# Tracing VectorE's attention work as one stream ahead of the weights' steps, with one product of the norm moved to ScalarE

## The chip, the cores and the metric

The kernel runs on one core of one Trainium2 chip. The metric is the device time of one execution in microseconds (us). Beside plain runs there is one profiled execution, whose trace is read here; its times are those of one execution. Engines are called as the profile calls them: PE is TensorE, DVE is VectorE, ACT is ScalarE, POOL is GpSimd and SP is SyncE, which issues most of the transfers.

## The reference: what is computed

A linear attention with a complex, normed gate runs over 768 time steps, for 4 batches and 8 heads of width 48. Its output is then the input of a mixture of four experts, whose results are summed with weights.

```python
mag = np.sqrt(a_re * a_re + a_im * a_im)
scale = np.minimum(mag, 0.999) / (mag + 1e-06)
a_re_n, a_im_n = (a_re * scale, a_im * scale)
for t in range(S):
    new_re = ar * S_re - ai * S_im
    new_im = ar * S_im + ai * S_re
    kv = np.einsum('bhd,bhe->bhde', k[:, :, t], v[:, :, t])
    S_re, S_im = (new_re + kv, new_im)
    y[:, :, t] = np.einsum('bhd,bhde->bhe', q[:, :, t], S_re)
...
p = d / (d.sum(-1, keepdims=True) + 1e-09)
for e in range(E):
    out += p[:, e:e + 1] * (np.maximum(x @ w1[e], 0.0) @ w2[e])
```

Here x is y with its heads side by side: 3072 rows of 384 numbers. An expert is 384 to 1024 to 384.

## The kernel before, in words

**Blocks.** The 3072 rows are worked off as NG = 12 blocks of G = 256 rows, each in two chunks of 128. A matrix product in fp32 is made of three products of high and low parts (hi x hi, lo x hi, hi x lo), so every x, hidden value and weight exists as a pair (xha and xla, hh and hl, whi and wlo).

**Two phases.** Up to about 614 us the experts 0 and 1 are applied to one block after the other (`moe1`, `mo.block`), and the attention of the next block is worked off between their steps. Then experts 2 and 3 run on blocks of 512 rows (`w1_full`, L739, and `w2_full`, L752) without any attention beside them. The change touches the first phase alone.

**A weight's step.** Each block takes eight steps of two weight tiles. `w1_step` makes 18 products into ph (L172); ScalarE makes hh from it (Relu, L181) and VectorE hl (L182). `w2_step` of the step before then makes 12 products into po (L191), from hh and hl. Ahead of each step k the function `between(k)` is called, which traces the pieces of the next block's attention; FIRST (L60) says with which step k the first of the three pieces comes.

**The attention of a block g.** Its gates are first normed (`norm`, L305 to L332): two Squares on ScalarE, their sum on VectorE, Ln, Exp and Identity on ScalarE, four products on VectorE (L326, L327, L328, L330) with a Square for a check between, and the product with the gates A. `prefix` (L334 to L356) then forms products of gates over the time steps of a chunk (pf, then sk and fm). The `head` of `finish` (L398) forms the squared magnitude of these products, its Ln and Exp, and Q (L408) out of q; the `tail` (L416) forms K (L422) out of k, with the inverse. `trip` (L428) writes Q or K to memory (q_d, k_d, L432) and reads it back turned round into Qst or Kst (L437), both on SP's queue.

TensorE's own pieces follow: turning K (ktp, L466, copied into KT), the increment of the state (dp, L484, then G on VectorE), the scores (sc, L496, out of Qst and Kst, then masked by VectorE into scs, L499), the values (yp, L510 and L515, copied into y by ScalarE, L522). At the end of a block `t_factors` copies TA and TB out of Qst (L444 to L447), and `rotate` (L534 to L537) turns the state G with them. For the blocks 0, 1 and 2 (XSEL = 3) the output is turned round on TensorE (xp, L546) and split into xha and xla straight from there (L159, L161); from block 3 on it goes through memory (`store_y`, `load_x`). Block 1 (and 0) is near: its K of the first chunk is turned on TensorE and copied into Kst by ScalarE (kp, L475, L476).

**What sets the order.** On each engine the instructions run in one fixed order. It is found by a scheduler that plays the program through when it is built; it starts from the order in which the code traces the instructions, and lets one pass another where its own clock says that this one is ready. In the kernel before, `front(g + 1)` (prefix, head, tail and the trips of a whole block) and `norm(g + 2)` are traced in one piece behind all eight steps of block g - 1. Tiles come from pools: gates A from two buffers, the temporaries of norm, prefix and Q from one pool of four (TMP), K from one.

Of the kernel before, what the change touches and what calls it, by code (L numbers as in the profile page):

```python
# [8 lines left out]
F32 = mybir.dt.float32  # L9
# [50 lines left out]
FIRST = {1: 5, 2: 4, 3: 3, 4: 2}  # L60
# [5 lines left out]
def fast_path(ctx, tc, qkP, aP, vP, probsP, w, out, flag):  # L66
# [16 lines left out]
    nc.vector.memset(neg1, -1.0)  # L83
    one1 = const.tile([P, 1], F32, name="one1")
# [137 lines left out]
    with ExitStack() as c1:  # L222
# [82 lines left out]
        def norm(g, A, parts=((0, SEG),), prev=(None, None)):  # L305
            s = tmp(f"s{g}")
            u = tmp(f"u{g}")
            for n, (lo, hi) in enumerate(parts):
# [15 lines left out]
                exp = nc.scalar.activation(y0, L, AF.Exp, scale=-0.5)
                idn = nc.scalar.activation(L, y0, AF.Identity, scale=-EPS, bias=one1)
                nc.vector.tensor_tensor(v, m2, y0, op=ALU.mult)  # L326
                nc.vector.scalar_tensor_tensor(v, v, 2.0 * EPS, y0, op0=ALU.add, op1=ALU.mult)  # L327
# [4 lines left out]
            return idn  # L332

        def prefix(g, A, cuts=(1, NS)):  # L334
            for i in range(1, SEG):
# [6 lines left out]
                nc.vector.tensor_tensor(x[:, 1], z[:, 1, 0], z[:, 0, 1], op=ALU.add)  # L342
            Al = A[:, :, SEG - 1, :]
            As = A.rearrange("p c i (j s) -> p c i j s", j=NJ)
            k = 1
            for lo, hi in zip(cuts, cuts[1:]):
                while k < hi:
# [3 lines left out]
                    cmul(Ak[:, :, :, k:], br, bi, [nb, k], f"sk{g}_{k}")  # L351
                    k *= 2
# [3 lines left out]
                yield  # L356
# [279 lines left out]
        nrm = norm(0, A[0], parts=halves)  # L636
        cuts = (1, NS // CG, NS)

        def front(g, A, qk):
            pre = prefix(g, A, cuts if g < NSEL else (1, NS))  # L640
            Q, K, head, tail = finish(g, A, qk)
            if g >= NSEL:
                next(pre, None)
                la = head(0, CG)
                ld = tail(0, CG)
                backs = [trip(f"{nm}_d{g}", X, st) for nm, X, st in (("q", Q, Qst), ("k", K, Kst))]
                return (Q, K), la, ld, [back() for back in backs][-1], None
# [10 lines left out]
            if g > 0:  # L658
                tail(0, 1)
# [318 lines left out]
```

## Time and profile before

| what | us |
|---|---|
| median of 3 runs | 1030.87 |
| lowest and highest run | 1030.55 and 1032.13 |
| profiled execution | 1026.41 |
| its span (first to last instruction) | 1024.5 |
| VectorE busy | 599.0 |
| ScalarE busy | 356.0 |

The profiled execution is 1.9 us longer than its span, and 4.46 us below the median. The granted TensorE clock over the span was 0.988 of full speed. A row of the timeline gives start, duration, engine, line, operation and tiles, and in brackets for how long its engine had been idle and on whom it waited; xN are neighbours of one kind put together. In the list of waits the three numbers are the sum, the number of waits and the longest. Names of tiles in the profile have no block number; which block a row belongs to comes from its place in the order.

### The profile page before, as it was taken

What the parts mean: (1) busy time and instruction counts of PE and PEld (TensorE: products, weight loads), DVE (VectorE), ACT (ScalarE), POOL (GpSimd) and SP (SyncE); (2) the same over time, 40 slices, a digit from 0 to 9 for tenths busy, and PEclk for the clock granted to TensorE, in tenths of its full rate; (3) what the DMA queues carried; (4) which work ended last, traced back from release to release, by engine and by line L of the source; (5) the groups of instructions that cost most, each with busy time, mean ns of one, the idle gap of its engine ahead of it and who ended that gap; (6) DMA issues with size and microseconds to landing.
All of it is one profiled execution on the core that took longest, in us unless ns stands there. A gap on an engine that the chain in (4) does not pass through costs nothing.

```text
span 1024.5 us, 16293 instructions
## 1 busy us (share of the span) xinstructions
PE 991.4 (97%) x6688; PEld 930.6 (91%) x6688; DVE 599.0 (58%) x1219; ACT 356.0 (35%) x642; POOL 34.3 (3%) x64
## 2 busy tenths in 40 slices
PE   4899999998999999999999999999999999999997
PEld 2799989898999999999999999989999999999996
DVE  7897979787888989788872264232232232321221
ACT  7655525353453536436242353121111111211110
POOL 5020000000000000000000000000000000000000
PEclk9899999998999999999999999999999999999999
DMA  9465265564736547384461592011030110100000
GB/s 325 137 131 148 86 163 132 132 161 125 191 116 167 142 130 187 123 201 121 120 167 29 187 337 94 1 62 62 1 123 1 31 62 1 62 1 1 32 1 34
DMA packets 74131, 110.78 MB, mean 108 GB/s; under 512 B 5248, under 2 KB 58544, under 8 KB 74048
## 3 DMA queue, kind: packets, MB, share of 16 engines
q1 hardware_dynamic: 69760, 94.53, 32.9%
q0 software_dynamic: 4288, 15.13, 5.0%
q8 instruction: 54, 0.88, 0.4%
q14 instruction: 29, 0.24, 0.1%
HBM read 73.72 MB, written 35.92 MB: 107 GB/s over the span
## 4 chain that ended last, share of the span: by engine, by line
PE 92%; DVE 2%; DMA 2%; issue 1%; ACT 1%; DVEq 0%; ACTq 0%
PE pob L752 20%; PE phb L739 19%; PE ph L172 19%; PE po L191 18%; PE sc L496 5%; PE dp L484 3%; PE yp L515 2%; PE yp L510 2%; PE ktp L466 1%; PE xp L546 1%; DMA Qst<-q_d 1%; DMA Kst<-k_d 1%; PE qp L368 0%; PE kp L368 0%; PE lp L142 0%
## 5 line engine op out<-in xcount | busy, mean ns | idle before, releaser
L745 DVE SCALAR_TENSOR_TENSOR hlb<-phb,hhb 128x512 fp32r<-128x512 f32 x96 | 66.3, 691 | 246.7 <-ACT hhb L744 246.7
L744 ACT ACTIVATE hhb<-phb 128x512 fp32r<-128x512 f32 x96 | 57.4, 598 | 313.3 <-PE phb L739 299.0
L191 PE MATMUL po<-whi,hh 128*128 128x384 f32 x384 | 129.4, 340 | 0.0
L752 PE MATMUL pob<-wlo,hhb 128*128 128x384 f32 x384 | 129.3, 337 | 0.0
L191 PE MATMUL po<-wlo,hh 128*128 128x384 f32 x384 | 129.1, 336 | 0.0
L752 PE MATMUL pob<-whi,hhb 128*128 128x384 f32 x384 | 128.9, 336 | 0.0
L191 PE MATMUL po<-whi,hl 128*128 128x384 f32 x384 | 123.9, 338 | 0.0
L752 PE MATMUL pob<-whi,hlb 128*128 128x384 f32 x384 | 117.8, 336 | 0.0
L172 PE MATMUL ph<-xha,whi 128*128 128x256 f32 x576 | 104.8, 288 | 0.6 <-ACT xha L159 0.6
L172 PE MATMUL ph<-xha,wlo 128*128 128x256 f32 x576 | 102.5, 284 | 0.0
L172 PE MATMUL ph<-xla,whi 128*128 128x256 f32 x576 | 102.4, 285 | 0.0
L181 ACT ACTIVATE hh<-ph 128x512 fp32r<-128x512 f32 x96 | 57.2, 596 | 130.0 <-PE ph L172 120.9
L182 DVE SCALAR_TENSOR_TENSOR hl<-ph,hh 128x512 fp32r<-128x512 f32 x96 | 66.0, 688 | 58.5 <-ACT hh L181 58.2
L739 PE MATMUL phb<-xhb,whi 128*128 128x512 f32 x288 | 91.8, 392 | 0.0
L172 PEld LDWEIGHTS ph<-xha,whi 128*128 128x128 f32 x576 | 87.2, 192 | 1.9 <-ACT xha L159 1.1
L172 PEld LDWEIGHTS ph<-xla,whi 128*128 128x128 f32 x576 | 83.2, 191 | 0.5 <-issue 0.5
L172 PEld LDWEIGHTS ph<-xha,wlo 128*128 128x128 f32 x576 | 83.5, 191 | 0.0
L739 PE MATMUL phb<-xlb,whi 128*128 128x512 f32 x288 | 83.4, 392 | 0.0
L739 PE MATMUL phb<-xhb,wlo 128*128 128x512 f32 x288 | 82.1, 393 | 0.0
L752 PEld LDWEIGHTS pob<-wlo,hhb 128*128 128x128 f32 x384 | 72.1, 188 | 3.5
L752 PEld LDWEIGHTS pob<-whi,hhb 128*128 128x128 f32 x384 | 72.1, 188 | 3.4
L191 PEld LDWEIGHTS po<-whi,hh 128*128 128x128 f32 x384 | 72.4, 189 | 0.6 <-issue 0.5
(165 smaller groups left out, 1585.3 us busy)
## 6 DMA issues: line engine op xcount, KB each, us to landing
wst<-w SPq DMA_DIRECT2D x25, 384.0 KB, 5.9
qk<-qkP SPq DMA_DIRECT2D x24, 384.0 KB, 6.8
acc_d<-acc POOLq DMA_DIRECT2D x24, 384.0 KB, 4.0
prev<-acc_d SPq DMA_DIRECT2D x24, 384.0 KB, 5.1
q_d<-Q SPq DMA_DIRECT2D x22, 387.0 KB, 3.5
Qst<-q_d SPq DMA_DIRECT2D x22, 387.0 KB, 5.8
A<-aP SPq DMA_DIRECT2D x22, 384.0 KB, 8.0
k_d<-K SPq DMA_DIRECT2D x20, 384.0 KB, 2.9
```

What stands on the lines that cost most here:

```text
L172: ins = nc.tensor.matmul(ph[:, u, :], wt[:, j * P:(j + 1) * P], xt[:, j, :], start=(n == 0), stop=(n == 3 * NJ - 1))
L181: wts["hh"] = nc.scalar.activation(hh, ph, AF.Relu)
L182: nc.vector.scalar_tensor_tensor(hl, ph, 0.0, hh, op0=ALU.max, op1=ALU.subtract)
L191: nc.tensor.matmul(po[t], ht[:, u, t * P:(t + 1) * P], wt[:, HD:], start=(i % FE == 0 and n == 0), stop=(i % FE == FE - 1 and n == 2))
L484: nc.tensor.matmul(d_ps[:, h, :], KT[:, h, :], vc[:, h * D:(h + 1) * D], start=True, stop=True)
L496: nc.tensor.matmul(s_ps[:, h, :], Kc[:, hf * 4 + h, :], Qc[:, hf * 4 + h, :], start=True, stop=True)
L510: ins = nc.tensor.matmul(yo, st[:, o:o + n], Qc[:, o // D, :], start=True, stop=False)
L515: ins = nc.tensor.matmul(yo, vc[:, o:o + n], sc[h // 4][:, h % 4, :], start=first, stop=True)
L739: nc.tensor.matmul(ph, wt[:, j * P:(j + 1) * P], xt[:, j, :], start=(n == 0), stop=(n == 3 * NJ - 1))
L744: nc.scalar.activation(hh, ph, AF.Relu)
L745: nc.vector.scalar_tensor_tensor(hl, ph, 0.0, hh, op0=ALU.max, op1=ALU.subtract)
L752: nc.tensor.matmul(po[t], ht[:, t * P:(t + 1) * P], wt[:, HD:], start=(i % FE == 0 and n == 0), stop=(i % FE == FE - 1 and n == 2))
```

## The change

It makes generators of `norm`, `prefix` and `front`: after each portion they yield a cost in us. `stream()` runs front(g) and norm(g + 1) for g = 1 to 11, one behind the other, and `advance(us, upto)` takes portions from it worth `us`, up to block `upto`. `between(k)` calls it ahead of every step of weights with STEP = 3.4 us, and with MORE on top at the three steps that carry a piece of attention. FIRST is raised by one for the blocks 2, 3 and 4. For the blocks in HALF (2 and 3) tail and K's trip are done chunk by chunk, which makes two writes and two reads of half the size out of each.

In the norm the factor 0.5 * CAP goes into Exp's bias. For g > 0 the two products m2 * y0 and (v + 2 EPS) * y0 of VectorE become a Square of y0 on ScalarE and one product of VectorE; the clamp becomes a max with -1, followed by the product with an Identity that has the other sign.

```diff
-FIRST = {1: 5, 2: 4, 3: 3, 4: 2}
+FIRST = {1: 5, 2: 5, 3: 4, 4: 3}
+STEP = 3.4
+MORE = (1.9, 1.9, 0.5)
+HALF = (2, 3)
...
-                exp = nc.scalar.activation(y0, L, AF.Exp, scale=-0.5)
-                idn = nc.scalar.activation(L, y0, AF.Identity, scale=-EPS, bias=one1)
-                nc.vector.tensor_tensor(v, m2, y0, op=ALU.mult)
-                nc.vector.scalar_tensor_tensor(v, v, 2.0 * EPS, y0, op0=ALU.add, op1=ALU.mult)
+                exp = nc.scalar.activation(y0, L, AF.Exp, scale=-0.5, bias=lnb)
+                if g == 0:
+                    nc.vector.tensor_tensor(v, m2, y0, op=ALU.mult)
+                    nc.vector.scalar_tensor_tensor(v, v, 4.0 / CAP ** 2, y0, op0=ALU.mult, op1=ALU.mult)
+                else:
+                    nc.scalar.activation(v, y0, AF.Square, scale=2.0 / CAP)
+                    nc.vector.tensor_tensor(v, m2, v, op=ALU.mult)
+                nc.scalar.activation(L, y0, AF.Identity, scale=2.0 * EPS / CAP, bias=neg1)
+                yield 0.95
                 nc.vector.scalar_tensor_tensor(y0, v, 3.0, y0, op0=ALU.subtract, op1=ALU.mult)
+                yield 0.95
                 nc.scalar.activation(v, v, AF.Square, bias=neg1, accum_out=st_w[:, col:col + 1])
-                nc.vector.scalar_tensor_tensor(y0, y0, -0.5 * CAP, L, op0=ALU.mult, op1=ALU.min)
+                nc.vector.scalar_tensor_tensor(y0, y0, -1.0, L, op0=ALU.max, op1=ALU.mult)
...
+            if g in HALF:
+                kb = []
+                for c in range(CG):
+                    last["dve"] = tail(c, c + 1)
+                    yield 2.7
+                    kb.append(trip(f"k_d{g}_{c}", K, Kst, c, c + 1))
+                    if c == 0:
+                        qb()
+                for back in kb:
+                    last["q"] = back()
...
+        def stream():
+            for g in range(1, NG):
+                qk = load_qk(g, last["q"])
+                if g + 1 < NG:
+                    A.append(load_a(g + 1, prev=last["q"]))
+                for r in front(g, A[g], qk):
+                    yield g, r
+                if g + 1 < NG:
+                    for r in norm(g + 1, A[g + 1]):
+                        yield g, r
+
+        work = stream()
+        spent = {"g": 1, "us": 0.0}
+
+        def advance(us, upto):
+            spent["us"] -= us
+            while spent["us"] < 0 and spent["g"] <= upto:
+                r = next(work, None)
+                if r is None:
+                    spent["g"] = NG
+                    return
+                spent["g"], cost = r
+                spent["us"] += cost
...
+            def between(k, g=g, first=first, end=end):
+                advance(STEP + (MORE[k - first] if first <= k <= end else 0.0), g + 1)
...
+                if g < NG and first <= k <= end:
+                    while g not in todo:
+                        advance(0.5, g)
...
-            if g + 1 < NG:
-                qk = load_qk(g + 1, landed)
-                if g + 2 < NG:
-                    A.append(load_a(g + 2, prev=landed))
-                QK, la, ld, landed, todo[g + 1] = front(g + 1, A[g + 1], qk)
-                if g + 1 >= NSEL:
-                    todo[g + 1] = attention(g + 1, QK)
-                if g + 2 < NG:
-                    norm(g + 2, A[g + 2])
```

TensorE's instructions stay the same in number. ScalarE gets 11 Squares, VectorE loses one product per norm and gains eight halves, and SP gets eight transfers more. How the order moves is shown at three places; in a name like hh0_7 the first number is the block and the second the step, in u23 it is temporary u2 of block 3 and in s4 temporary s of block 4.

ScalarE, where block 1's first scores need Kst. Before:

```order
L324 ACTIVATE u2_773<-s2_772 128x768
L444 ACTIVATE TA_164<-Qst_160 48x8
L445 ACTIVATE TA_164<-Qst_160 48x8
L325 ACTIVATE s2_772<-u2_773,one1_85 128x768
L446 ACTIVATE TB_165<-Qst_160 48x8
L447 ACTIVATE TB_165<-Qst_160 48x8
L476 ACTIVATE Kst_161<-kp1_0_0_988 112x4x128
L476 ACTIVATE Kst_161<-kp1_0_4_994 112x4x128
L181 ACTIVATE hh0_7_1239<-ph0_7_1220 128x512
```

The same place now:

```order
L330 ACTIVATE u2_967<-s2_966,lnb_85 128x768
L459 ACTIVATE TA_166<-Qst_162 48x8
L460 ACTIVATE TA_166<-Qst_162 48x8
L461 ACTIVATE TB_167<-Qst_162 48x8
L335 ACTIVATE u2_967<-u2_967 128x768
L337 ACTIVATE s2_966<-u2_967,neg1_83 128x768
L462 ACTIVATE TB_167<-Qst_162 48x8
L491 ACTIVATE Kst_163<-kp1_0_0_981 112x4x128
L491 ACTIVATE Kst_163<-kp1_0_4_987 112x4x128
L186 ACTIVATE hh0_7_1267<-ph0_7_1248 128x512
```

The norm's new Square and its Identity stand behind the first TB copy, where the Identity stood ahead of it.

ScalarE, where block 2's x is copied into xha. Before:

```order
L159 ACTIVATE xha2_1733<-xp2_1_1689 128x3x128
L405 ACTIVATE u23_1781<-s23_1780,a2b_89 128x24x16
L411 ACTIVATE Q3_1782<-A3_1258 128x12
L313 ACTIVATE s4_1871<-A4_1777 128x768
L314 ACTIVATE s4_1871<-A4_1777 128x768
L405 ACTIVATE u23_1781<-s23_1780,a2b_89 128x24x16
L406 ACTIVATE u23_1781<-u23_1781,a2e_91 128x24x16
L181 ACTIVATE hh2_0_1904<-ph2_0_1885 128x512
L406 ACTIVATE u23_1781<-u23_1781,a2e_91 128x24x16
L323 ACTIVATE s4_1871<-s4_1871,m2b_87 128x768
L181 ACTIVATE hh2_1_1945<-ph2_1_1926 128x512
L324 ACTIVATE u4_1872<-s4_1871 128x768
```

The same place now:

```order
L420 ACTIVATE u23_1647<-s23_1646,a2b_91 128x24x16
L426 ACTIVATE Q3_1648<-A3_1054 128x12
L318 ACTIVATE s4_2039<-A4_1643 128x768
L319 ACTIVATE s4_2039<-A4_1643 128x768
L420 ACTIVATE u23_1647<-s23_1646,a2b_91 128x24x16
L164 ACTIVATE xha2_1779<-xp2_1_1770 128x3x128
L421 ACTIVATE u23_1647<-u23_1647,a2e_93 128x24x16 x2
L329 ACTIVATE s4_2039<-s4_2039,m2b_89 128x768
L330 ACTIVATE u4_2040<-s4_2039,lnb_85 128x768
L335 ACTIVATE u4_2040<-u4_2040 128x768
L337 ACTIVATE s4_2039<-u4_2040,neg1_83 128x768
L186 ACTIVATE hh2_0_1853<-ph2_0_1834 128x512
```

Two Ln, the copy into Q3 and two Squares have moved ahead of the second half of xha2, and the norm's whole run ahead of hh2_0.

VectorE, where K4 is made. Before:

```order
L182 SCALAR_TENSOR_TENSOR hl3_0_2429<-ph3_0_2409,hh3_0_2428 128x512
L418 TENSOR_TENSOR u24_2305<-s24_2304,u24_2305 128x768
L419 SCALAR_TENSOR_TENSOR u24_2305<-u24_2305 128x768
L326 TENSOR_TENSOR u5_2396<-s5_2395,u5_2396 128x768
L420 TENSOR_TENSOR u24_2305<-qk4_2298,u24_2305 128x768
L182 SCALAR_TENSOR_TENSOR hl3_1_2470<-ph3_1_2450,hh3_1_2469 128x512
L327 SCALAR_TENSOR_TENSOR u5_2396<-u5_2396 128x768
L422 TENSOR_TENSOR K4_2307<-A4_1777,u24_2305 128x8x6x16 x2
```

The same place now:

```order
L187 SCALAR_TENSOR_TENSOR hl2_7_2343<-ph2_7_2323,hh2_7_2342 128x512
L551 TENSOR_TENSOR G3_1_2266<-G3_1_2266,TA_166 112x384
L336 TENSOR_TENSOR u5_2529<-s5_2528,u5_2529 128x768
L437 TENSOR_TENSOR K4_2207<-A4_1643,u24_2205 128x8x6x16 x2
L552 TENSOR_TENSOR G3_1_2266<-G3_1_2266,P2_165 112x384
L187 SCALAR_TENSOR_TENSOR hl3_0_2398<-ph3_0_2378,hh3_0_2397 128x512
L339 SCALAR_TENSOR_TENSOR u5_2529<-u5_2529 128x768
L187 SCALAR_TENSOR_TENSOR hl3_1_2452<-ph3_1_2432,hh3_1_2451 128x512
```

K4 has moved from behind hl3_1 to ahead of hl3_0. In the same way the two halves of K2 now stand on both sides of hl1_3 (it stood behind hl1_4), and K3 stands ahead of hl2_0 (it stood behind hl2_2).

More of the change, by code (lines that the diff above doesn't have):

```diff
@@ L635, in fast_path @@
         A.append(load_a(1))
-        nrm = norm(0, A[0], parts=halves)
+        for _ in norm(0, A[0], parts=halves):
+            pass
         cuts = (1, NS // CG, NS)
+        todo, last = {}, {}
         def front(g, A, qk):
@@ L655, in front, with ahead @@
-            next(pre)
-            la = head(1, CG)
-            landed = next(pieces)
-            if g > 0:
-                tail(0, 1)
-            ld = tail(1, CG)
-            return next(pieces) if g == 0 else None, la, ld, landed, pieces
-        x, todo = {}, {}
-        x[0], la, ld, landed, todo[0] = front(0, A[0], qk)
-        norm(1, A[1], prev=(la, ld))
+            def ahead():
+                for r in pre:
+                    if r == 0:
+                        return
+                    yield r
@@ new lines, in front @@
+            if g < NSEL:
+                pieces = near_attention(g, (Q, K))
+                yield from ahead()
+                yield 1.8
+                head(0, 1)
+                yield 1.6
+                if g == 0:
+                    next(pieces)
+                    tail(0, 1)
+                    next(pieces)
+                yield from ahead()
+                yield 2.0
+                last["act"] = head(1, CG)
+                yield 1.6
+                last["q"] = next(pieces)
+                if g > 0:
+                    tail(0, 1)
+                    yield 2.7
+                last["dve"] = tail(1, CG)
+                yield 2.7
+                todo[g] = pieces
+                return
@@ new lines, in front @@
+            yield from ahead()
+            yield 3.9
+            last["act"] = head(0, CG)
+            yield 3.0
+            qb = trip(f"q_d{g}", Q, Qst)
+            if g in HALF:
+                kb = []
+                for c in range(CG):
+                    last["dve"] = tail(c, c + 1)
+                    yield 2.7
+                    kb.append(trip(f"k_d{g}_{c}", K, Kst, c, c + 1))
[3 more added lines that the diff above has]
+                    last["q"] = back()
+            else:
+                last["dve"] = tail(0, CG)
+                yield 4.8
+                kb = trip(f"k_d{g}", K, Kst)
+                qb()
+                last["q"] = kb()
@@ L666, in fast_path @@
+            todo[g] = attention(g, (Q, K))
+        x = {}
+        for _ in front(0, A[0], qk):
+            pass
+        x[0] = next(todo[0])
+        for _ in norm(1, A[1], prev=(last["act"], last["dve"])):
+            pass
         for i in range(NPRE):
@@ new lines, in fast_path @@
+            first = FIRST.get(g, 2)
+            end = first + len(MORE) - 1
+            def between(k, g=g, first=first, end=end):
+                advance(STEP + (MORE[k - first] if first <= k <= end else 0.0), g + 1)
+                if g == 1:
+                    for i in range(NPRE + 2 * k, min(NPRE + 2 * k + 2, NF1)):
+                        add_w(i, wts["hh"] if k else wts["x"])
+                if g < NG and first <= k <= end:
+                    while g not in todo:
+                        advance(0.5, g)
+                    r = next(todo[g], None)
+                    if r is not None:
+                        x[g] = split_x(g, r) if g < NSEL else r
+                if k == max(end, nk - 1) and g in x and g >= NSEL:
+                    x[g] = split_x(g, x[g])
@@ L713, in fast_path @@
+            moe1(g - 1, *x.pop(g - 1), between)
+            for k in range(nk, end + 1):
+                between(k)
     for i in range(NF1, NF1 + AHEAD):
```

45 lines of the change are left out of this document (11 added, 34 removed).

## Prediction

> **What bounds the kernel now.** I read the page first, then the list of what TensorE waits for, then TensorE's own rows at those places, and last the rows of VectorE and ScalarE ahead of them.
>
> ```profile
> span 1024.5 us, 16293 instructions
> PE 991.4 (97%) x6688; PEld 930.6 (91%) x6688; DVE 599.0 (58%) x1219; ACT 356.0 (35%) x642; POOL 34.3 (3%) x64
> ...
> DVE  7897979787888989788872264232232232321221
> ```
>
> TensorE (PE) is busy for 97% of the span, so a gain can only come from the rest and from its clock. VectorE (DVE) is at 58% over all, but near nine tenths in the first half, where the attention is worked off. What TensorE waits for:
>
> ```profile
> PE lp L142 <- DMA wst<-w: 9.2, 1, 9.2
> PE qp L368 <- DVE Q L408: 6.4, 1, 6.4
> PE sc L496 <- issue: 5.9, 3, 2.7
> ...
> PE sc L496 <- ACT Kst L476: 1.2, 1, 1.2
> PE sc L496 <- DMA Kst<-k_d: 0.9, 1, 0.9
> ...
> ```
>
> The first two rows are the start (first weights, first Q), which the change leaves as it is. Nearly all the rest is one instruction, the score product sc, which needs K turned round in the tile Kst. These are the waits for g = 1, 2, 3, 4 and 5, in brackets the idle time before each row:
>
> ```profile
> 91.97 2.05 PE L496 MATMUL sc<-Qst,Kst 112*128 112x128 f32 x16 [1.22 <-ACT Kst L476]
> ...
> 142.79 0.46 PE L496 MATMUL sc<-Qst,Kst 112*128 112x128 f32 x2 [1.72 <-issue]
> ...
> 186.43 0.35 PE L496 MATMUL sc<-Qst,Kst 112*128 112x128 f32 x1 [1.50 <-issue]
> ...
> 233.57 0.77 PE L496 MATMUL sc<-Qst,Kst 112*128 112x128 f32 x2 [2.67 <-issue]
> ...
> 279.72 0.46 PE L496 MATMUL sc<-Qst,Kst 112*128 112x128 f32 x2 [0.91 <-DMA Kst<-k_d]
> ```
>
> Behind three of them the clock falls. Of each window the columns are: stretch, length, TensorE's busy time, then the other engines, then granted clock, DMA share and GB/s.
>
> ```profile
> 88.69:92.10 3.41, 2.19 (x13) 1.87 (x13) 0.65 (x1) 2.11 (x6) 0.00 (x0) 1.00 1.05 270
> ...
> 143.30:146.72 3.42, 3.42 (x19) 2.87 (x17) 1.64 (x5) 0.00 (x0) 0.00 (x0) 0.50 0.66 254
> ...
> 187.68:191.09 3.41, 3.41 (x17) 3.41 (x17) 2.70 (x7) 0.58 (x1) 0.54 (x1) 0.50 0.54 209
> ...
> 232.05:235.46 3.41, 1.89 (x9) 1.92 (x10) 0.04 (x1) 0.00 (x0) 0.00 (x0) 0.50 1.03 376
> 235.46:238.87 3.41, 3.41 (x17) 2.83 (x17) 2.63 (x6) 0.00 (x0) 0.00 (x0) 0.50 0.06 23
> ```
>
> So the waits of g = 2, 3 and 4 are paid twice: once as idle time, and once as half of the busy time at clock 0.50: 3.42/2 = 1.71, 3.41/2 = 1.70, (1.89 + 3.41)/2 = 2.65. The wait of 1.22 at g = 1 left the clock at 1.00.
>
> **What is removed.** K2, K3 and K4 are the last link; these are VectorE's rows of their last two products, and the transfers from there to Kst, with their times from issue to landing.
>
> ```profile
> 130.42 1.82 DVE L422 TENSOR_TENSOR K<-A,u 128x768 f32<-128x768 f32 x2
> ...
> 174.20 1.82 DVE L422 TENSOR_TENSOR K<-A,u 128x768 f32<-128x768 f32 x2
> ...
> 222.15 1.82 DVE L422 TENSOR_TENSOR K<-A,u 128x768 f32<-128x768 f32 x2
> ```
>
> ```profile
> Kst<-k_d SPq DMA_DIRECT2D x20, 384.0 KB, 5.8
> ...
> Qst<-q_d SPq DMA_DIRECT2D x2, 193.5 KB, 3.7
> ```
>
> K ends at 132.24, 176.02 and 223.97, and sc follows 10.55, 10.41 and 9.60 later. The gain of each block is how much earlier K comes on VectorE, less how much earlier sc itself now stands on TensorE, and it has to exceed the wait. Earlier on VectorE is read against the hl product (L182) beside which K now stands:
>
> ```profile
> 126.19 0.68 DVE L182 SCALAR_TENSOR_TENSOR hl<-ph,hh 128x512 fp32r<-128x512 f32 x1
> ...
> 167.36 0.69 DVE L182 SCALAR_TENSOR_TENSOR hl<-ph,hh 128x512 fp32r<-128x512 f32 x1 [0.29 <-ACT hh L181]
> ...
> 211.57 0.69 DVE L182 SCALAR_TENSOR_TENSOR hl<-ph,hh 128x512 fp32r<-128x512 f32 x1
> ```
>
> These are hl1_3, hl2_0 and hl2_7. What TensorE has less ahead of sc is priced by the chain's rows of 18 ph and 12 po products:
>
> ```profile
> 400.89 2.15 PE ph L172 x18
> ...
> 408.29 2.15 PE po L191 x12
> ```
>
> - g = 2. In the new order half of K2 stands ahead of hl1_3 and the other half right behind it, where K2 ended 5.4 behind hl1_3's end. The first half is about 6.1 earlier, and a half read lands like the row of 193.5 KB, 2.1 sooner: 8.2. On TensorE 12 ph and 15 po fewer stand ahead of sc: 1.43 + 2.69 = 4.1. Left 4.1, over the 1.72 that is waited.
> - g = 3. K3, in halves too, stands ahead of hl2_0, where it ended 176.02 - 167.36 = 8.7 behind its start; with about 0.9 for its own place that is 9.6 earlier. 18 ph and 11 po fewer: 2.15 + 1.97 = 4.1. Left 5.5, over 1.50.
> - g = 4. K4 now stands behind hl2_7 with one G product and one u5 product between: 0.55 + 0.95 + 1.82 = 3.3 behind its end, where it was 223.97 - 212.26 = 11.7: 8.4 earlier. 26 ph and 12 po fewer: 3.1 + 2.15 = 5.25. Left 3.2, over 2.67 by 0.5 only; this is the weakest of the three.
> - g = 5 gains 4.1 and gives back 3.3: between 0 and 0.91 of its wait goes; I take 0.5, the middle.
>
> So 1.72 + 1.71, 1.50 + 1.70, 2.67 + 2.65 and 0.5 go: 12.45. FIRST is raised, which by itself would place sc later; the new order shows it earlier all the same, because the whole work of VectorE is traced ahead.
>
> **What the arithmetic of the norm brings.** Per norm one VectorE product goes and one ScalarE Square of the same width comes:
>
> ```profile
> L327 DVE SCALAR_TENSOR_TENSOR u<-u 128x768 f32<-128x768 f32 x11 | 10.5, 953 | 0.1
> ...
> L313 ACT ACTIVATE s<-A 128x768 f32<-128x768 f32 x11 | 9.2, 837 | 0.0
> ```
>
> That is 10.5 us off VectorE and 9.2 us onto ScalarE. From 290 us on TensorE waits for neither (the list above has nothing there), so both are covered by its matmuls; before 290 us the order above holds them already. Without the cover the Square would cost 0.84 per block. The eight more transfers on SP are the halves of g = 2 and 3; their queue has room, and they count with the landing above.
>
> **What is added.** Three places, all from the new order of ScalarE and VectorE.
>
> First sc of g = 1. ScalarE's rows there:
>
> ```profile
> 88.79 0.94 ACT L325 ACTIVATE s<-u,one 128x768 f32<-128x768 f32 x1
> ...
> 91.00 0.21 ACT L446 ACTIVATE TB<-Qst 48x8 f32<-48x8 f32 x1 [1.27 <-DMA Qst<-q_d]
> 91.35 1.05 ACT L476 ACTIVATE Kst<-kp 112x512 f32<-112x512 f32 x2
> ```
>
> The Identity of the norm ran at 88.79, inside the time in which ScalarE waited for the landing at 91.00. Now Square and Identity stand behind a TB copy that needs this landing, and ahead of the Kst copies. By their rows they take 0.84 (the Square, as the row of L313) + 0.94 = 1.78; a following start overlaps each end by about 0.1, so I take 1.58 (bounds 0, if the landing comes earlier by as much, and 1.78).
>
> Second hl1_0. Five products that stood behind it now stand ahead (two of 0.83, three of 0.55) and two of 0.95 are gone from there:
>
> ```profile
> L302 DVE TENSOR_TENSOR A<-fm_1a,fm_1b 128x651 f32<-128x651 f32 x10 | 8.3, 829 | 0.1
> ...
> L422 DVE TENSOR_TENSOR K<-A,u 128x384 f32<-128x384 f32 x8 | 4.1, 552 | 0.0
> ...
> L181 ACT ACTIVATE hh<-ph 128x512 fp32r<-128x512 f32 x96 | 57.2, 596 | 130.0 <-PE ph L172 120.9
> ```
>
> 1.66 + 1.66 - 1.9 = 1.4 later. The next ph of TensorE covers 2.15 - 0.60 - 0.69 = 0.9 (ph less hh and hl), which leaves 0.5 (bounds 0 and 1.4).
>
> Third ph2_0, the first product of block 2, which needs xha2, the second half of its x:
>
> ```profile
> 163.01 0.49 ACT L159 ACTIVATE xha<-xp 128x384 fp32r<-128x384 f32 x1
> ...
> 163.55 0.62 ACT L405 ACTIVATE u<-s,a2b 128x384 f32<-128x384 f32 x1
> ...
> 166.15 0.60 ACT L406 ACTIVATE u<-u,a2e 128x384 f32<-128x384 f32 x1
> ...
> 170.10 0.85 ACT L324 ACTIVATE u<-s 128x768 f32<-128x768 f32 x1 [0.96 <-DMA q_d<-Q]
> ```
>
> From 163.55 to 166.15 ran Ln, the copy into Q3, both Squares of s4 and the second Ln, 2.60 in all, behind xha2. Now they stand ahead of it. Eight po between the last yp and xp save some 0.2 of the wait for y there: 2.4 (bounds 0, if ScalarE is through with them before xp is done, and 4.6, if hh2_0 is held as well by Exp, Square and Identity, which now stand ahead of it). VectorE is late at the same place: ten half products of K3 and one of u4 (10 x 0.55 + 0.95 = 6.5) stand ahead of hl2_0, for Q3 and the sum of s4, which took 2.8: 3.7 more, of which the 2.4 cover all but 1.3.
>
> What does the clock do there? TensorE idles about 3.1 in one piece, longer than any of the three waits above behind which it was at 0.50, so I take one spell of 3.41, 1.7. TensorE is then slower by as much, and VectorE's 1.3 are hidden by it. For g = 1 the wait of 2.8 falls on two windows, and I take no spell.
>
> [...]
>
> **The sum.** -12.45 + 1.58 + 0.5 + 2.4 + 1.7 = -6.27. The profiled execution took 1026.41 (span 1024.5 and 1.9 around it), which gives 1020.1 with a profile. It lies 4.46 below the median of the runs, 1030.87; the median should then be 1030.87 - 6.27 = 1024.6.
>
> **The rivals.** About 0.2% (2.06 us) is what a measurement of this kernel can tell from no change.
>
> - *Nothing is lost at block 2.* If ScalarE has its run done before xp ends, the 2.4 and the 1.7 go: -10.4, 1020.5. For it: ScalarE is busy for only 35%, and its Squares of g = 3 now stand ahead of the copy of y. Against it: Ln, Q copy and Squares stand behind acc, which waits for the eight po. Chance 0.14.
> - *A landing stays last.* If K4 comes only as much earlier as sc does, its wait and its spell stay, 5.32, and the change does at the dearest place not what it says: -0.95, 1029.9. For it: only 0.5 of spare at g = 4, and the three times from K to sc above differ by 0.95. Against it: the same spare is 2.4 and 4.0 at the other two. Chance 0.17.
> - *ScalarE becomes the bound at the start of blocks (slower).* The norm's run (Ln, Exp, the new Square, Identity) stands ahead of hh or xha. If it also holds block 3, 4 and so on as at block 2, each costs 2.4 + 1.7 = 4.1; two further blocks decide: -6.27 + 8.2 = +1.9, three +6.0. I take two and a little: 1033.0. For it: Exp waits for the buffer that Q leaves only when its transfer has landed (the row at 170.10). Against it: from g = 3 on x is loaded through y_d and split long before the block, so only hh is left, which has most of a step of 4.3. Chance 0.16.
>
> **How the numbers follow.** My forecast keeps 0.53. Faster by over 0.2%: 0.53 + 0.14 = 0.67; within: 0.17; slower: 0.16. The range leaves out the slower rival alone: from 1018.4, where all 12.45 go and nothing is added, to 1031.0, where the landing stays last and g = 1 and hl1_0 take their upper bounds (0.2 and 0.9 more).
>
> **What would show it.** Right: sc of g = 2, 3 and 4 without a bracket and no half clock at 143, 187 and 232; a wait of about 2.8 at sc of g = 1 on Kst; about 3 at ph2_0 on xha with one spell behind it; a VectorE busy time lower by 10, a ScalarE busy time higher by 9. Wrong: a bracket of over 1 us at sc of g = 4; new waits of po or ph on hh or hl in blocks 3 to 5; no wait at ph2_0. That the later blocks gain from VectorE's 10 us would show as a shorter stretch behind 290 us, which I do not expect.

## The result, and the profile after

The first four runs of the changed kernel had a median of 1020.69 us (1019.04 to 1022.82), beside 1031.46 (1030.55 to 1032.13) in four runs of the kernel before: ratio 0.9916, 95% interval [0.9894, 0.9938]. Measured again on one chip, with 8 and 19 runs, the medians were 1020.27 and 1025.09: ratio 0.9952 [0.9933, 0.9971]. The change makes the kernel faster by about 5 us; the first four runs of the kernel before lay at the upper end of its spread. In 29 runs on one chip that kernel took from 1021.39 to 1032.74, and the time goes with the granted clock: 1032.74 at a clock of 0.986, 1024.24 at 0.994. One window of 3.41 us at half clock lowers the mean clock of 1024.5 us by 0.0017 and costs up to 1.7 us, an estimate from half of its length; a spread that is mainly the number of such windows that a run meets would fit this, but windows were seen in the profiled executions alone. Two runs of the experiments took far longer at a low granted clock, 1092.43 of e11 (0.848) and 2273.31 of e6b (0.433), and the ratios and intervals leave them out.

The profiled executions of the two kernels are 1026.41 and 1021.09, 5.3 apart. The page of the changed kernel:

```profile
span 1019.3 us, 16332 instructions
...
PE 986.1 (97%) x6688; PEld 926.6 (91%) x6688; DVE 591.0 (58%) x1219; ACT 363.7 (36%) x653; POOL 34.4 (3%) x64
```

VectorE is 8.0 us less busy and ScalarE 7.7 more, where 10 and 9 were forecast. VectorE's instructions are 1219 as before: 11 products of the norm go, one constant comes, and the halves bring ten more, not eight (five products in each of two blocks). What TensorE waits for behind the first weights and the first Q (9.1 and 6.3, about as before):

```profile
PE sc L511 <- ACT Kst L491: 2.8, 2, 2.5
PE ph L177 <- ACT xha L164: 2.3, 1, 2.3
PE sc L511 <- DMA Kst<-k_d: 1.4, 1, 1.4
...
PE lp L147 <- ACT wlo L151: 1.4, 1, 1.4
PE po L196 <- ACT hh L186: 0.9, 1, 0.9
PE po L196 <- DVE hl L187: 0.4, 1, 0.4
```

The row "sc <- issue: 5.9" is gone. In its place stand the three waits that the prediction added (Kst, xha, hl) and one it had not (hh). In TensorE's timeline these are sc of g = 1, a po of block 1, sc of g = 2 without a bracket, the first ph of block 2, sc of g = 3 (none), a po of block 3, and sc of g = 4 (none) and 5:

```profile
93.19 3.25 PE L511 MATMUL sc<-Qst,Kst 112*128 112x128 f32 x16 [2.53 <-ACT Kst L491]
...
120.22 0.62 PE L196 MATMUL po<-whi,hl 128*128 128x384 f32 x2 [0.37 <-DVE hl L187]
...
140.90 2.02 PE L511 MATMUL sc<-Qst,Kst 112*128 112x128 f32 x16
...
165.44 1.00 PE L177 MATMUL ph<-xha,whi 128*128 128x256 f32 x3 [2.28 <-ACT xha L164]
...
184.09 2.02 PE L511 MATMUL sc<-Qst,Kst 112*128 112x128 f32 x16
...
211.91 0.44 PE L196 MATMUL po<-whi,hh 128*128 128x384 f32 x1 [0.86 <-ACT hh L186]
...
226.20 2.02 PE L511 MATMUL sc<-Qst,Kst 112*128 112x128 f32 x16
...
271.73 2.02 PE L511 MATMUL sc<-Qst,Kst 112*128 112x128 f32 x16 [1.41 <-DMA Kst<-k_d]
```

Behind the first bracket and that of ph the clock is at half for one window each:

```profile
93.81:97.22 3.41, 3.41 (x21) 3.19 (x22) 3.41 (x4) 1.32 (x3) 0.00 (x0) 0.50 0.00 0
...
165.49:168.90 3.41, 3.41 (x16) 3.41 (x17) 3.41 (x10) 3.35 (x5) 0.00 (x0) 0.50 0.64 186
```

ScalarE's rows at the two places show the order that the prediction spoke of. At g = 1, Square and Identity run behind a TB copy that waited for Qst, and ahead of Kst; at block 2, Ln and Squares run ahead of the second half of xha (the rows of both Ln, and of xha):

```profile
90.51 0.21 ACT L461 ACTIVATE TB<-Qst 48x8 f32<-48x8 f32 x1 [1.95 <-DMA Qst<-q_d]
90.75 0.84 ACT L335 ACTIVATE u<-u 128x768 f32<-128x768 f32 x1
91.50 0.92 ACT L337 ACTIVATE s<-u,neg 128x768 f32<-128x768 f32 x1
...
92.56 1.05 ACT L491 ACTIVATE Kst<-kp 112x512 f32<-112x512 f32 x2
...
162.34 0.60 ACT L420 ACTIVATE u<-s,a2b 128x384 f32<-128x384 f32 x1
...
164.41 0.61 ACT L420 ACTIVATE u<-s,a2b 128x384 f32<-128x384 f32 x1
164.92 0.47 ACT L164 ACTIVATE xha<-xp 128x384 fp32r<-128x384 f32 x1
```

So the time went, in the main, where the forecast had it. Which part of the change moved it was not, as the experiments show.

### The profile page after: what moved, and what is told of

Read it like the earlier page. It is cut to its first block, busy times and chain, and to the rows that moved or that the text cites. A ratio compares the mean times of both kernels' runs of the same rounds, so it can differ in the third digit from the quotient of the medians.

```text
span 1019.3 us, 16332 instructions
## 1 busy us (share of the span) xinstructions
PE 986.1 (97%) x6688; PEld 926.6 (91%) x6688; DVE 591.0 (58%) x1219; ACT 363.7 (36%) x653; POOL 34.4 (3%) x64
## 4 chain that ended last, share of the span: by engine, by line
PE 85%; DMA 5%; DVE 4%; ACT 3%; POOL 1%; issue 1%; SPq 0%; ACTq 0%; POOLq 0%
PE pob L821 20%; PE phb L808 20%; PE ph L177 17%; PE po L196 16%; PE sc L511 5%; PE dp L499 2%; DMA q_d<-Q 2%; PE yp L530 2%; PE yp L525 2%; PE ktp L481 1%; PE xp L561 1%; DMA Kst<-k_d 1%; DMA Qst<-q_d 1%; DMA mask_d<-mask 1%; PE kp L383 1%
```

## The experiments

All ratios are to the kernel before, measured beside it on the same chip; e13, e14, e15 and e6b ran on another chip than the other experiments. "Waits" is the sum of what TensorE waits for between the start and 614 us in the one profile (the rows of sc, ph, po, xp and dp in the list of waits), "half" the number of windows at half clock there.

| kernel | parts | ratio, 95% interval | median | waits | half |
|---|---|---|---|---|---|
| before | none | 1 | 1025.09 to 1031.46 | 10.0 | 4 |
| after | all | 0.9916 [0.9894, 0.9938] | 1020.69 | 9.2 | 2 |
| after_again | all | 0.9952 [0.9933, 0.9971] | 1020.27 | 8.9 | 0 |
| e1 | norm | 0.9996 [0.9976, 1.0016] | 1025.63 | 13.7 | 1 |
| e11 | stream | 1.0029 [1.0008, 1.0051] | 1028.36 | 14.2 | 2 |
| e8 | halves | 0.9904 [0.9881, 0.9926] | 1015.17 | 4.5 | 0 |
| e13 | halves of the way through memory alone | 0.9969 [0.9952, 0.9985] | 1023.65 | 8.5 | 1 |
| e14 | norm, halves | 0.9929 [0.9903, 0.9954] | 1018.93 | 7.7 | 2 |
| e2 | stream, FIRST, halves | 0.9947 [0.9925, 0.9969] | 1021.35 | 8.2 | 1 |
| e3 | stream, FIRST, norm | 0.9989 [0.9969, 1.0010] | 1024.89 | 11.6 | 2 |
| e6a | all, Kst first | 0.9898 [0.9865, 0.9932] | 1015.88 | 6.6 | 1 |
| e6b | all, xha of block 2 first | 0.9957 [0.9942, 0.9973] | 1022.78 | 8.3 | 3 |
| e9 | all, Kst first, halves to 5 | 0.9889 [0.9867, 0.9912] | 1013.75 | 4.9 | 0 |
| e15 | halves to 5 | 0.9906 [0.9882, 0.9930] | 1015.92 | 4.9 | 0 |

My theory going in (A) was that the shorter norm moves K ahead of sc, because the kernel before with the new norm alone is scheduled with K3 and K4 at the places of the changed kernel, and the changed kernel with the old norm is not. The rival (B) was the prediction's own: the stream does it.

**e1, the norm alone.**

```diff
-                exp = nc.scalar.activation(y0, L, AF.Exp, scale=-0.5)
+                exp = nc.scalar.activation(y0, L, AF.Exp, scale=-0.5, bias=lnb)
...
-                nc.vector.scalar_tensor_tensor(v, v, 2.0 * EPS, y0, op0=ALU.add, op1=ALU.mult)
+                    nc.scalar.activation(v, y0, AF.Square, scale=2.0 / CAP)
+                    nc.vector.tensor_tensor(v, m2, v, op=ALU.mult)
...
```

Identity and clamp change here as in the whole change.

> The kernel before with the new arithmetic of the norm alone (one VectorE product less, one ScalarE Square more per norm); no stream, old FIRST, no halves. In its order K3 stands ahead of hl2_0 and K4 ahead of hl3_0, as in the changed kernel, and K2 behind hl1_3. Theory A, the shorter norm is what moves K ahead of sc: the waits of sc at g = 3 and 4 (1.50 and 2.67) and their half-clock windows are gone, a wait of 1 to 3 us at the first ph of block 2 comes, ratio 0.990 to 0.997. Theory B, the stream is what brings the gain: the waits stay within 0.5 us of before, ratio 0.998 to 1.002.

Measured 0.9996 [0.9976, 1.0016]. The order moved as expected, and the time did not. At g = 3 TensorE comes to sc 0.65 earlier and K3 ends only 0.38 earlier. At g = 2 K2 ends 1.8 earlier, but sc follows it by 13.13 us, where it was 10.55. Only at g = 4 is something won: K4 ends 3.8 earlier, and TensorE comes 1.3 earlier. The waits for g = 1 to 4 are 2.39, 3.10, 1.82 and 1.02:

```profile
93.81 1.38 PE L502 MATMUL sc<-Qst,Kst 112*128 112x128 f32 x10 [2.39 <-ACT Kst L482]
...
143.54 1.78 PE L502 MATMUL sc<-Qst,Kst 112*128 112x128 f32 x10 [3.10 <-issue]
...
186.10 2.02 PE L502 MATMUL sc<-Qst,Kst 112*128 112x128 f32 x16 [1.82 <-issue]
...
230.63 1.58 PE L502 MATMUL sc<-Qst,Kst 112*128 112x128 f32 x12 [1.02 <-issue]
```

The wait at g = 4 fell from 2.67; those at g = 1, 2 and 3 grew. The wait that A expected at the first ph of block 2 came (1.90), with new ones at a po (1.14) and a dp (0.58) of that stretch. Theory A falls.

**e2, the change with the old norm.**

```diff
-                    nc.scalar.activation(v, y0, AF.Square, scale=2.0 / CAP)
-                    nc.vector.tensor_tensor(v, m2, v, op=ALU.mult)
+                nc.vector.tensor_tensor(v, m2, y0, op=ALU.mult)
+                nc.vector.scalar_tensor_tensor(v, v, 4.0 / CAP ** 2, y0, op0=ALU.mult, op1=ALU.mult)
```

The norm has its old number of instructions on each engine again; the new constants and the clamp stay. The same holds for e11.

> The changed kernel with the VectorE product put back in the norm in place of ScalarE's Square; stream, FIRST and halves stay. In its order K3 stands between hl2_1 and hl2_3 and K4 behind hl3_1, where the kernel before has them, and the copy xha of block 2 stands ahead of the Squares of block 4. Theory A: sc at g = 4 waits 2 to 3 us again with half clock behind it, no wait at the first ph of block 2, ratio 0.994 to 1.001. Theory B: the gain stays, ratio 0.988 to 0.993.

Measured 0.9947 [0.9925, 0.9969], at the lower edge of A's range, near the middle of neither, and not to be told from the whole change (0.9952). K4 stands where it stood before, yet sc at g = 4 waits only 0.9 ("issue"), and sc of g = 2 and 3 not at all. The longest wait is now that of sc at g = 5, 2.2, with a window at half clock behind it:

```profile
PE sc L507 <- DMA Kst<-k_d: 2.5, 2, 2.2
PE sc L507 <- ACT Kst L487: 1.5, 1, 1.5
...
PE sc L507 <- issue: 0.9, 1, 0.9
```

**e3, the change without halves.**

```diff
-HALF = (2, 3)
+HALF = ()
```

> The changed kernel with K of blocks 2 and 3 made and carried whole (HALF empty). Theory A, the halves matter little, since the second half of K2 stands where the whole K2 stands now, right behind hl1_3: sc at g = 2 waits 0 to 0.6 us, at g = 3 nothing, ratio within 0.002 of the changed kernel (0.990 to 0.994). Rival, the halves carry g = 2 and 3: both waits come back at 1.5 us or more with a half-clock window each, 3 to 6 us, ratio 0.994 to 0.998.

Measured 0.9989 [0.9969, 1.0010]: the gain is gone. It is not gone in the way that the rival said. sc at g = 2 waits 0.45 and at g = 3 nothing; what is new is a wait of 2.30 at the first ph of block 3, with half clock behind it:

```profile
215.53 0.68 PE L177 MATMUL ph<-xha,whi 128*128 128x256 f32 x3 [2.30 <-ACT xha L164]
```

So stream, FIRST and norm all but free sc at g = 2, 3 and 4 without the halves, but TensorE's waits sum to 11.6 us, more than the 10.0 before.

That both e2 and e3 missed left a third theory: the halves bring the gain by themselves (D), or only with the stream (C).

**after_again, the change once more,** as the measure beside the next three.

> The changed kernel once more, beside 5 rounds of the kernel before on one chip, as the measure for the other runs. The runs of the kernel before spread from 1021.39 to 1032.74 on one chip and go with the granted clock (0.986 to 0.994), so a median of four runs can lie some us off. Theory: the profiled difference (5.3) is nearer to the truth than that of the first medians (10.8): ratio 0.992 to 0.996.

Measured 0.9952, within that range. Its profile (1018.17) has nearly the same waits as the first one, one more at a po of block 2 (0.86, on hl), and no window at half clock.

**e8, the halves alone.**

```diff
+HALF = (2, 3)
...
                 la = head(0, CG)
+                if g in HALF:
+                    qb = trip(f"q_d{g}", Q, Qst)
+                    kb = []
+                    for c in range(CG):
+                        ld = tail(c, c + 1)
+                        kb.append(trip(f"k_d{g}_{c}", K, Kst, c, c + 1))
+                        if c == 0:
+                            qb()
+                    return (Q, K), la, ld, [back() for back in kb][-1], None
```

> The kernel before with nothing but K of blocks 2 and 3 in halves. In its order the second half of K2 stands where all of K2 stood, behind hl1_4, and sc of g = 2 stands 9 ph and 11 po earlier, 3.0 us. Theory C, the halves help only together with the stream: a read begins behind the write of the second half, so 2.1 us of landing are gained against 3.0 us that sc comes earlier; sc at g = 2 waits 1.5 to 3 us, ratio 0.997 to 1.003. Theory D, the halves alone bring the gain: no wait of over 0.5 us at g = 2 and 3, ratio 0.992 to 0.996.

Measured 0.9904 [0.9881, 0.9926]: theory D, and more than it asked for. It is faster than the whole change (0.9952 [0.9933, 0.9971]). Its profiled execution took 1015.31, 11.1 less than that of the kernel before; TensorE's waits are 5.5 shorter, and the four windows at half clock, worth 6.1 by the estimate of half their busy time, are gone. What TensorE still waits for behind the start:

```profile
PE xp L547 <- ACT y L523: 1.4, 2, 0.7
PE sc L497 <- DMA Kst<-k_d: 1.3, 4, 0.5
PE sc L497 <- issue: 0.6, 1, 0.6
PE ph L173 <- ACT xha L160: 0.6, 1, 0.6
PE sc L497 <- ACT Kst L477: 0.6, 1, 0.6
```

How it works is seen on SP's queue. First the kernel before at g = 2. Real and imaginary part of K2 are two writes and two reads, here the writes together and each read by itself:

```profile
131.39 1.25 SPq L432 DMA_DIRECT2D k_d<-K  x2
...
134.52 0.32 SPq L437 DMA_DIRECT2D Kst<-k_d  x1
...
136.48 0.32 SPq L437 DMA_DIRECT2D Kst<-k_d  x1
```

The writes landed at 134.05 and 136.46, and the second read left 0.02 behind the second of them. The reads took 5.6 and 6.2 us to land.

Now e8, VectorE's first half of K2, SP's rows and sc itself:

```profile
128.26 1.02 DVE L423 TENSOR_TENSOR K<-A,u 128x384 f32<-128x384 f32 x2
```

```profile
128.83 0.91 SPq L433 DMA_DIRECT2D k_d<-K  x2
132.92 0.83 SPq L438 DMA_DIRECT2D Kst<-k_d  x2
133.81 0.99 SPq L433 DMA_DIRECT2D k_d<-K  x2
137.37 0.84 SPq L438 DMA_DIRECT2D Kst<-k_d  x2
```

```profile
137.56 2.02 PE L497 MATMUL sc<-Qst,Kst 112*128 112x128 f32 x16
```

The reads of the first half stand ahead of the writes of the second and take 3.2 and 3.5 us to land. sc of the first chunk starts before the reads of the second half have landed: it follows the end of the first half of K2, 129.28, by 8.28, without waiting, where it followed the whole K2 by 10.55. My expectation for C had this read behind the second write; that was wrong. Rows of x2 hold two transfers, so 2.27 us, the length of the pair of whole reads, is no time of issuing: each of these reads takes 0.32 to 0.41 to issue, whole or half. My expectation for e13 still read it so. The edit also traces Q's write ahead of K, but it stays where it was on SP's queue (121.67 before, 121.31 here).

**e13, only the way through memory in halves.**

```diff
+                    ld = tail(0, CG)
                     qb = trip(f"q_d{g}", Q, Qst)
                     kb = []
                     for c in range(CG):
-                        ld = tail(c, c + 1)
                         kb.append(trip(f"k_d{g}_{c}", K, Kst, c, c + 1))
```

Against e8, the whole K is made ahead of the two trips.

> The kernel before with K of blocks 2 and 3 made whole as before, and only its way through memory in halves (two writes and two reads of 192 KB each). TensorE's and VectorE's order are those of the kernel before, word for word. Theory L, what counts is the landing: the half read takes about 0.8 us to issue and 3.4 to 3.7 to land, where the whole one took 2.3 and 5.8, and sc of the first chunk needs the first half alone: the waits of 1.72 and 1.50 at g = 2 and 3 fall under 0.5 us, ratio 0.991 to 0.997. Theory V, what counts is that VectorE has half of K ready sooner: with K whole the waits stay at 1 us or more, ratio 0.997 to 1.002.

Measured 0.9969 [0.9952, 0.9985]: a part. TensorE and VectorE are ordered as before, and the waits at g = 2 and 3 fall from 1.72 and 1.50 to 0.64 and 0.34, the first a little above what L asked; at g = 4, where K goes whole, the wait is 3.21 for 2.67:

```profile
141.85 2.02 PE L497 MATMUL sc<-Qst,Kst 112*128 112x128 f32 x16 [0.64 <-issue]
...
182.78 2.05 PE L497 MATMUL sc<-Qst,Kst 112*128 112x128 f32 x16 [0.34 <-DMA Kst<-k_d]
...
228.92 1.42 PE L497 MATMUL sc<-Qst,Kst 112*128 112x128 f32 x6 [3.21 <-issue]
```

So halves of the way alone are worth about 3 us of the 10. This is no clean price of landing, for here the reads of the first half stand behind all four writes: at g = 2 they take 4.7 and 4.8 us to land, not the 3.4 to 3.7 of L. At g = 3 sc starts right behind the landing of the third read (182.73), which carries part of the second half, and at g = 2 it starts 0.09 behind it too; why, when the first half had landed 1.4 to 1.5 us before, I have not found. The rest comes with VectorE's halves, that is, with half of K ready sooner and with the order that follows from it. At g = 4, where K is whole in e8 too, sc waits 0.65 there: it follows K4 by 9.84, about as before (9.60), but K4 ends 9.6 us earlier and TensorE comes to sc only 7.3 earlier. What in the new order does this I have not isolated.

**e11, the stream alone,** so e2 without halves and with the old FIRST.

```diff
-HALF = (2, 3)
+HALF = ()
-FIRST = {1: 5, 2: 5, 3: 4, 4: 3}
+FIRST = {1: 5, 2: 4, 3: 3, 4: 2}
```

> The changed kernel with the old norm, the old FIRST and no halves, so with the stream alone. In its order K2 stands one hl product earlier (behind hl1_3) and sc of g = 2 has 9 po less ahead; g = 3, 4 and 5 stand as in the kernel before. Theory C, the stream moves K2 alone: 4.3 us less 1.6 us is more than the wait of 1.72, so sc at g = 2 waits no more, at g = 3 and 4 it does (1 to 3 us), ratio 0.995 to 0.999. Theory D, the stream is worth nothing without the rest: 0.999 to 1.002.

Measured 1.0029 [1.0008, 1.0051]: slower. C falls, D nearly holds. K2 stands one hl earlier, but sc at g = 2 still waits 1.99, and those at g = 3, 4 and 5 wait 2.10, 3.33 and 1.47. Theory B falls with it.

**e14, norm and halves without the stream:** the edits of e1 and of e8 together.

> The kernel before with the new norm and the halves, without the stream and with the old FIRST. In its order sc of g = 2 stands 26 ph and 23 po earlier than before, and ScalarE has Square and Identity ahead of the Kst copies of block 1. Theory X, the new norm is what gives back a part of the halves' gain: sc at g = 1 waits 2.0 to 2.6 us on Kst, sc at g = 2 waits 1 to 4 us, ratio 0.994 to 0.999. Theory Y, the stream is what gives it back: without it the ratio is that of the halves alone, 0.988 to 0.992.

Measured 0.9929 [0.9903, 0.9954], between X and Y. The waits are X's: sc at g = 1 waits 2.72 on Kst, at g = 2 1.12 and at g = 3 2.10, where e8 has 0.57, none and 0.29. In all its waits are 3.2 longer than in e8 (7.7 and 4.5), and its ratio is higher by 0.0025, with an interval that overlaps that of e8. So by its waits the norm gives back some of what the halves bring; the times do not show it beyond noise.

**e6a, Kst first at block 1.**

```diff
+            if g == 1:
+                behind(ta, state["kst", g])
```

The first TA copy stands behind the last Kst copy of the first chunk.

> The changed kernel with the TA and TB copies of block 1 put behind the Kst copies on ScalarE, so that Kst no longer stands behind the norm's Square and Identity there. Theory A, that order is what sc at g = 1 waits for: its wait falls from 2.53 to at most 0.5 us and the half-clock window at 93.8 us goes, together 3.5 to 4.2 us, ratio 0.986 to 0.989. Rival, the landing of Qst ends last in any case: 1.0 to 1.5 us of wait stay, and the gain over the changed kernel is 1 to 3 us.

Measured 0.9898 [0.9865, 0.9932], A with a ratio just above its range: the wait at g = 1 falls from 2.53 to 0.22. The half clock behind it is gone too, but the second profile of the changed kernel had none there either, behind a wait of 2.16. ScalarE's rows show that Square and Identity now run while it has nothing else, and Kst is ready before Qst (at 89.32; the TB copy still waits for Qst until 91.14):

```profile
86.68 0.85 ACT L335 ACTIVATE u<-u 128x768 f32<-128x768 f32 x1
87.43 0.92 ACT L337 ACTIVATE s<-u,neg 128x768 f32<-128x768 f32 x1
88.26 1.06 ACT L494 ACTIVATE Kst<-kp 112x512 f32<-112x512 f32 x2
```

**e9, the same and halves for blocks 4 and 5.**

```diff
-HALF = (2, 3)
+HALF = (2, 3, 4, 5)
```

> The changed kernel with TA and TB behind the Kst copies at block 1, and with halves for the blocks 4 and 5 as well. It adds to the kernel with TA and TB moved (ratio 0.9898) that the wait of sc at g = 5 on the landing of Kst (1.04 us there) should go, with the half-clock window behind it: ratio 0.986 to 0.990. Rival, sc of g = 5 only comes earlier by as much (17 ph fewer ahead of it, 2.0 us): the wait stays and the ratio is that of the kernel without these halves.

Measured 0.9889 [0.9867, 0.9912]: sc waits nowhere any more, and what is left behind the start are 2.3 at ph of block 2, 1.4 at xp and 1.2 at po. Against e6a the ratio does not tell it apart.

**e15, the halves alone, to block 5.** The same edit of HALF in e8.

> The kernel before with halves for the blocks 2 to 5 and nothing else of the change. It takes from the kernel with halves for 2 and 3 (0.9904) the waits of sc at g = 4 and 5 (0.65 and 0.33 us): ratio 0.987 to 0.991, faster than both kernels. Rival: sc comes earlier by as much, the ratio stays within 0.001 of 0.9904.

Measured 0.9906 [0.9882, 0.9930]. That lies in the range of the theory and in that of the rival, and it is not faster than e8. The first chunk's sc at g = 4 and 5 waits no more, as the theory had it, though it stands 5 ph and 12 po earlier at g = 4. But the second chunk's sc at g = 4 now waits 1.02 for the second half of K4, a little more than was gained.

**e6b, the second half of block 2's xha first.**

```diff
+                if g == 4:
+                    after_x2(ins[0], sq)
...
+                    if g == 3:
+                        after_x2(ln)
```

`after_x2` puts the Squares of s4 and the Ln of u23 behind the second half of xha2.

> The changed kernel with the Ln of block 3 and the two Squares of block 4 put behind the second half of the copy xha2 on ScalarE. The scheduler then moves K3 from ahead of hl2_0 to behind hl2_1, and sc of g = 3 comes 18 ph and 7 po later. Theory, the wait of 2.28 at the first ph of block 2 is the price of that ScalarE order alone: it falls to 0.5 to 0.7, no wait of over 0.6 comes at sc of g = 3, ratio 0.990 to 0.994. Rival, the later K3 costs as much again at sc of g = 3 or at an hl: ratio 0.994 to 0.998.

Measured 0.9957 [0.9942, 0.9973], the rival's ratio at another place. The wait at ph falls from 2.28 to 0.58, and one of 1.79 comes, not at g = 3 but at sc of g = 4, which the changed kernel has without a wait. So here the wait was moved to another place; it was not saved.

Four kernels, e8, e15, e6a and e9, are faster than the kernel before, and than the changed one as measured again (their intervals end below 0.9933, those of e15 and e6a only just); against its first four runs (0.9916) they overlap. The slowest runs of e8 and e9, 1016.56 and 1014.99, lie below the fastest of the changed kernel measured beside them, 1017.93. The four are not told apart among themselves. FIRST by itself, or the change with the old FIRST, was not run.

## Why the prediction came out right, and where its reasons did not

**The terms.** The forecast was -6.27; measured are -5.3 in the first profile and -4.8 by the medians on one chip (1025.09 to 1020.27); the second profile, 1018.17, is 8.2 below that of the kernel before. Term by term in the first profile, the windows at half clock again priced at half their busy time:

| term | forecast | measured |
|---|---|---|
| sc at g = 2, 3, 4, idle | -5.89 | -5.89 |
| their half-clock windows | -6.06 | -6.06 |
| sc at g = 5 | -0.5 | +0.50 (0.91 to 1.41) |
| sc at g = 1 | +1.58 | +1.31 (1.22 to 2.53) |
| a po of block 1 on hl | +0.5 | +0.37 |
| first ph of block 2 | +2.4 | +1.70 (0.58 to 2.28) |
| po of block 3 on hh | none | +0.86 |
| new half-clock windows | +1.7 | +3.4 (two) |

The measured column sums to -3.81, 1.5 short of the -5.3. The stretch from 60 us to the end of the first phase, before and now, shows where the rest is (stretch, length, TensorE's busy time, then the other engines):

```profile
60.00:614.40 554.40, 545.10 (x4352) 529.99 (x4351) 438.12 (x929) 245.33 (x449) 16.96 (x28) 0.99 0.56 151
```

```profile
60.00:609.20 549.20, 540.90 (x4351) 526.98 (x4350) 430.90 (x928) 252.03 (x458) 16.96 (x28) 0.99 0.57 152
```

TensorE's idle time falls from 9.3 to 8.3, about as the rows of the table have it. Its busy time falls by 4.2, of which the windows at half clock make 2.7 by the estimate of half their busy time. The other 1.5 is busy time outside these windows, and its cause is open.

**Luck.** That -6.27 lies so near to -5.3 is in part luck. The terms were off by 2.46 on balance (+1.00 at g = 5, +1.7 of clock, +0.86 at hh, -1.10 at the other three), and 1.5 us that no term held took most of it back. The median came out at 1020.69, 3.9 below the 1024.6 of the forecast, which stood on three runs at the upper end of the spread (1030.87, against 1025.09 in 19 runs).

**Right.** The waits of g = 2, 3 and 4 are gone, with their windows. The three new waits stand at the places and on the tiles that the order told, with 2.53 for 2.80, 0.37 for 0.5, and 2.28 for about 3.0. VectorE's hl2_0 is hidden behind the half clock there, as forecast. In the second profile, without half clock, it shows, with 0.86 for the 1.3 that the spell was to hide:

```profile
170.45 0.61 PE L196 MATMUL po<-whi,hl 128*128 128x384 f32 x2 [0.86 <-DVE hl L187]
```

The rival of ScalarE as a bound in every block, and with it one of the signs of being wrong, shows in small, 0.86 on hh at block 3; e3 shows what it can be, 2.30 with half clock behind it.

**Wrong: what makes it.** The step that failed is the sentence that the order shows sc earlier "because the whole work of VectorE is traced ahead". The stream alone moves K2 and nothing behind it, and alone makes the kernel slower by 0.8 to 5.2 us (e11, the interval). HALF alone frees sc of g = 2 and 3 (e8: none and 0.29) and is worth 0.0096 of the time, twice the whole change as measured again; without it the change gains nothing that can be told from noise (e3). The prediction counted HALF with 2.1 us of landing at g = 2 and with the place of K2's first half, as help for a gain that it put down to the stream. It is not the only way to free these places: stream, FIRST and norm together leave 0.45 and nothing there (e3), but the time is lost again at other places. So a wait that goes at sc is not yet a gain.

**Wrong: the norm counted at nothing.** Its time on the engines is indeed hidden; measured alone it changes nothing beyond noise (e1, 0.9996), nor does it with stream and halves (0.9952 with, 0.9947 without). But it is not neutral in its parts. It is the new norm by which the scheduler puts K3 and K4, and sc with them, earlier, and by which Square and Identity come to stand ahead of Kst: the old norm has a wait of 1.47 there (e2), the new one 2.4 to 2.7 (e1, e3, e14). "Before 290 us the order above holds them already" hid this: an order that both parts made was booked on one of them.

**Wrong: g = 5.** K5 is carried whole, and its way took as long as ever: sc followed K by 9.6 to 10.6 us at g = 2 to 5 in the kernel before, and K5 by 10.1 now. I expected VectorE's 4.1 to outdo TensorE's 3.3; the wait grew by 0.50, and it was 1.06 in the second profile, 0.15 more than before.

**The clock.** The forecast of one new window was two in the first profile and none in the second, with nearly the same waits, so this term could not be had from the size of a wait. In the first profile and in that of the kernel before the stretches at half clock are one or two times 3.41 us long, and their starts lie whole numbers of that length apart: 187.68 - 143.30 = 44.38 and 232.05 - 187.68 = 44.37 in the kernel before, 13 lengths each, and 165.49 - 93.81 = 71.68 in the changed kernel, 21 lengths. In the second profile no half clock between the start and 614 us marks where such windows begin. Laid as here, which is my estimate, the wait of 2.28 (161.34 to 163.62) falls on both sides of a border:

```profile
159.70:163.11 3.41, 1.64 (x14) 1.45 (x12) 1.83 (x4) 3.41 (x8) 0.54 (x1) 1.00 0.84 275
163.11:166.52 3.41, 2.90 (x24) 2.90 (x25) 3.41 (x9) 3.35 (x7) 0.00 (x0) 1.00 0.77 234
```

and the clock stays at 1.00, where in the first profile the same wait lay in one window, with half clock in the next:

```profile
162.07:165.49 3.42, 1.14 (x11) 0.95 (x10) 1.83 (x5) 3.42 (x8) 0.54 (x1) 1.00 0.88 289
```

So half clock followed a window with 1.14 of 3.42 us busy here, and one with 1.69 of 3.41 in the kernel before (139.89 to 143.30).

Half of the busy time was my estimate of what such a window costs. The rows of ph at block 2 show somewhat less. First at half clock, then at full clock:

```profile
166.88 0.84 PE L177 MATMUL ph<-xha,whi 128*128 128x256 f32 x3
167.52 0.84 PE L177 MATMUL ph<-xha,wlo 128*128 128x256 f32 x3
...
170.28 0.52 PE L177 MATMUL ph<-xha,whi 128*128 128x256 f32 x3
170.64 0.52 PE L177 MATMUL ph<-xha,wlo 128*128 128x256 f32 x3
```

Three products follow the three before them by 0.64 us and by 0.36, so a window of 3.41 filled with them loses about 1.5, not 1.7.

## What to carry to other kernels

Ask of each wait which piece of data ends it, and whether the first user needs all of it: K cut in two on its whole way, from the engine that makes it to the tile that is read, was worth 10 us, where the stream or the norm alone, which only move its maker, were worth nothing. When a change makes a scheduler reorder, an order that looks better on one engine can be worse on another, so book each move to the edit that causes it by scheduling each edit alone. A wait that goes may come back elsewhere, so count all of them. And a row that holds two transfers says nothing of the time of one: look at each. And where runs of one kernel differ by the clock, a median of four is no measure for half a per cent.

## What the runs showed of the hardware that was not expected

- A wait of one size may or may not cost a window at half clock: that of 2.28 at ph of block 2 did in the first profile of the changed kernel and did not in the second. Windows with 0.89 and 1.14 us of 3.42 busy were followed by one in the first; of those between 1.6 and 2.3 some were (1.69, 1.92 and 2.27 in the kernel before) and some were not (2.19 there, at 88.69, and 1.64 and 1.86 in stretches of 3.41 of the second profile of the changed kernel). In these traces busy time alone does not decide it.
- One read of K took 0.32 us to issue on SP's queue whole (the kernel before, g = 2) and 0.32 to 0.41 as a half (e8, first half); what the half saved was landing, 3.2 and 3.5 us there for 5.6 and 6.2. Behind four writes, as in e13, the halves took 4.7 and 4.8.
- The way of one whole K from VectorE to sc is not constant: 9.6 to 10.6 us in the kernel before, 13.1 at g = 2 of e1.
